# An S4 convolution with a gated GELU block on one core: the y table of a step as one product on VectorE, and a new order of all work

## The chip, the cores and the metric

The kernel runs on one core of a Trainium2 chip. The core has five engines with their own queues: TensorE (PE, matrix products into PSUM), VectorE (DVE), ScalarE (ACT), GpSimd (POOL) and SyncE (SP, which here issues most of the transfers). The metric is the device time of one execution in microseconds (us); lower is better. Three executions of the kernel before took 823.56, 824.63 and 826.21 us, with a median of 824.63 us.

## The reference

An input u of 2048 tokens and 448 channels goes through two blocks, each behind a layer norm that is scaled and shifted by rows computed from a vector c. Cut to what matters:

```python
# S4 block: a convolution kernel per channel, from 256 complex modes
logdA = exp(log_dt)[:, None] * (A_re + 1j * A_im)
P = exp(logdA[:, :, None] * l)                      # l = 0..2047
K = einsum("dn,dnl,dn->dl", Cc, P, dB).real         # 448 x 2048
y = irfft(rfft(u_padded) * rfft(K_padded))[:L] + u * Dskip
x = x + ga * y
# gated block
h = layernorm(x) * (1 + cb) + sb
x = x + gb * ((gelu(h @ w_gate) * (h @ w_up)) @ w_down)
```

The costly part of the first block is K: 448 x 2048 values, each a sum over 256 complex modes of an exponential with a decay and an angle. The costly part of the second is three matrix products of 448 by 1792.

## The kernel before, in words

**The tables of K.** The time l is split as l = 64 l1 + l2. For a mode the power then factors into an x table (over the 32 values of l1) and a y table (over the 64 values of l2); K of a channel is the product of the two, summed over the modes. The work goes in 56 steps of 8 channels. In a step s:

- `exps` (lines 759 to 795) makes the magnitudes: a matrix product and an exponential on ScalarE give `mx` for two steps (line 775) and `my` for one (line 793, 1024 elements: 2 halves of modes, 8 channels, 64 values of l2).
- `angles` (lines 797 to 841) makes sine and cosine. Matrix products of bf16 pieces (line 806) leave the angle in turns, with whole turns taken off by a large constant, in PSUM; ScalarE makes the sine (line 819) and the cosine. In the first 28 steps the cosine comes from a second set of angles with a quarter turn added (`anc`, line 830); in the other 28 it is the sine of the angle's absolute value minus a quarter turn (lines 811 or 814, then 823). Both lie in one tile `fg`, for x and for y. The y angles cover 32 values of l2 only; the other half of the 64 is carried by the two halves of `my` and by signs.
- `mults` (lines 844 to 867) makes the tables on VectorE: `tx` is one product of 1024 elements (line 855). `ty` has three: the cosine part, 1024 elements (line 859), the sine part of the first half with its sign turned, 512 elements (line 862), and the sine part of the second half, 512 elements (line 863).
- `kgen` (lines 871 to 890) has 64 small matrix products, line 886, `tx` as weights and 64 columns of `ty` as the moving operand, into `kg`.
- `ktail` then copies `kg` out into `ke` (`kev`), applies a first stage of the Fourier transform (line 911) and collects the result in `ako` (`kout`). Copies out of PSUM, which may run on ScalarE or VectorE, go through the helper `cp` and show as line 585 (ScalarE) or 587 (VectorE).
- The rows that the products of lines 769, 788 and 806 take as weights come from DRAM for seven steps at a time, by `load_lt` (line 751).

Beside the steps run: the preparation of the modes for four groups of 112 channels (`prep`), the norm and transform of u (`u_norm_a`, `u_stage_b`), and for two of three groups of channels the product of the transforms and its inverse (`k_fft`, lines 1189 to 1213, with constants loaded by line 1181). The third group's transforms (`t_fft`) come after the last step.

**The gated block.** `conv_out` adds the convolution, norms it and transposes it; `gate_up` makes gate and up with fp16 pieces (lines 1588 and 1594), GELU (1601) and the product (1608); `down_first` (line 1663) and `down` (line 1694) make the last product.

**What sets the order.** The program is not written in the order in which it runs. Each piece of work is a `Task` with its engine or engines, a cost in us, the tasks it depends on and the buffers it takes. `Plan.order` is a list planner: it keeps a clock for each engine, finds the engine that can start something first, and gives it, among the tasks that can start by then or shortly after, the one of lowest priority value in `PRIO`. `PRIO` has one number for each of some 2000 tasks. A task with two engines (copies out of PSUM) goes to the one that ends it first. A change of ScalarE's function table costs `TABLE` = 1.3 us in the plan, a hand-over between engines `HOP` = 0.3 us, and all transfers share one pipe of 280 GB/s. The planner runs when the program is built; its result is a fixed order for each engine and each queue, in which each instruction waits for what it needs. So a number in the planner never runs on the chip; it only moves instructions within their queues.

Of the kernel before, what the change touches and what calls it, by code (L numbers as in the profile page):

```python
# [11 lines left out]
FT = mybir.dt.float32  # L12
# [3 lines left out]
AF = mybir.ActivationFunctionType  # L16
OP = mybir.AluOpType
# [20 lines left out]
WS = 256.0  # L38
PRIO = {
    "anc": (-1293.256, -3578.895, -353.961, -872.318, -460.437, -1921.377, -2404.991, -2215.805, 191.288, -32.981, -202.691,  # L40
        -2647.333, -1933.83, -670.792, -192.873, -616.144, -80.921, -1549.964, -2941.687, -671.342, -2001.879, -1132.111,
        -71.643, -27.945, -252.965, -1535.421, -769.379, -1539.333),
    "ang": (-63.859, -7.725, -30.71, 0.169, 7.925, 11.195, 9.268, 21.779, 22.824, 25.594, 26.183, 26.493, 28.144, 28.708,
# [5 lines left out]
    "c.ai": (-2663.528,),  # L49
    "c.ak": (171.218,),  # L50
    "c.au": (-4200.533,),
    "c.c": (-933.544,),
    "c.ea": (5422.27,),
    "c.id": (-147.248,),
    "c.ih": (1109.11,),
    "c.ld": (-3220.083,),
    "c.rd": (2966.135,),
    "co.adde": (-84.218, -1452.145, -2417.83, -1409.323),
    "co.addl": (-57.786, 676.69, 1533.586, 31.466),
    "co.addx": (-1428.076, -8.045, 2531.362, 3088.204, -2578.892, 2089.375, -473.92, 382.232, 1219.977, -537.482, 53.247,  # L60
        1140.208),
    "co.c2": (553.038, 3254.154, 1888.633, -595.169, 1726.527, -906.573, 4858.759, 40.493, -1400.834, 27.831, 1819.503,
        -161.366),
    "co.h": (336.967, 2645.855, 1868.777, -2126.118),
    "co.h2": (-650.973, 75.139, 637.166, -1259.465, -8.18, -1329.599, 13.947, -1333.575, 5413.552, -346.388, 3335.76, 1270.416),
    "co.l": (-2527.984, -675.661, 723.03, 3544.242),
    "co.l2": (1124.467, 1797.664, 1246.234, 626.032, 529.696, 1269.558, 529.646, -451.738, -1181.182, 2221.273, 450.372,
        434.525),
    "co.mme": (4028.037, 3822.614, -709.965, -3597.943),
    "co.mml": (-661.981, 33.929, 1870.772, -68.779),  # L70
    "co.mmx": (348.366, -620.465, 1977.413, 2997.574, -279.998, 3308.134, 630.569, 742.671, -398.692, -288.917, -47.372,
        2601.845),
    "co.n": (-637.705, -78.904, -2172.773, -124.152),
    "co.nx": (-1207.602, 1920.968, -700.888, 0.561, -1307.228, -3639.226, 373.628, -35.065, -24.718, 34.24, 1425.966, -6133.847),
    "co.rc": (1435.224, -2102.468, 1120.167, 435.885),
    "co.rcx": (864.192, -118.249, 3179.105),
    "co.rt": (-668.81, -40.146, 1435.174, -1099.33),
    "co.rtx": (-306.185, -80.314, 5310.55),
    "co.t": (-701.977, -362.858, 11.547, -251.511),
    "co.t2": (-1003.663, 677.507, 490.748, 1973.53, -67.147, -1774.919, -292.344, -677.791, 196.69, -3024.797, -183.214, 15.548),  # L80
    "cos": (47.809, 4338.677, -1916.389, -1985.479, 48.84, 450.345, -228.642, 1373.754, -1635.183, -2125.449, -2951.945,
        139.392, -590.217, -1488.189, -465.57, -115.397, -138.704, 2366.141, 654.971, 78.486, 63.259, -3501.827, 365.129,
        -594.75, 843.446, -2481.552, 3748.658, 338.746),
    "cos2": (-186.283, -458.553, -28.501, -1467.414, -186.383, 305.735, -4173.308, 2676.943, -903.314, -2645.906, -803.054,
        147.233, 61.493, -902.839, -698.019, 3.975, 96.182, 670.288, 4882.18, -890.924, -903.013, 1267.647, -38.519, 1684.391,
        654.047, -1006.703, 490.617, -217.831),
    "d.hi": (-16.935, -885.611, 1072.565, -1866.073, 565.92, -545.207, 277.832),
    "d.ld": (-1036.334, 594.218, -5342.563, -1512.808, 784.13, 1290.275, -992.387),
    "d.lo": (-1950.133, -1401.218, -2174.946, -390.7, -1260.169, -6.416, 1957.309),
    "d0": (-1079.999,),  # L90
    "dn": (-3573.259, -323.838, 1692.909, 1720.273),
    "dn.k0": (1759.554, 521.981, -3993.33),
    "dn.k2": (-1082.302, -1650.584, -6237.94),
    "dn.k3": (-388.073, 2717.888, 2751.692),
    "dn.r": (586.912, 103.145, 2224.364, -500.948),
# [1797 lines left out]
```

## Time and profile before

| | |
|---|---|
| median of three executions | 824.63 us |
| profiled execution | 822.29 us |
| its span, first to last instruction | 820.5 us |
| TensorE busy | 744.8 us, 91% |
| VectorE busy | 609.2 us, 74% |
| ScalarE busy | 464.4 us, 57% |
| mean granted clock of TensorE | 0.972 |
| moved by DMA | 136.78 MB, mean 167 GB/s |

The shares are means over stages with different limits: loads and preparation up to about 40 us, the 56 steps up to about 371 us, the last transforms and the way into the gated block up to about 420 us, and the gated block from there on. A row of the table of stretches gives, for each engine, its busy time in the stretch and the number of instructions; a row of a group gives the line of the program, the engine, what is written and read, the count, the busy time, the mean length of one in ns, and the engine's idle time just ahead with what ended it. The chain that ended last follows the work back from the last instruction, at each step to what released it.

### The profile page before, as it was taken

To read this page: it belongs to the slowest core of one execution; us is meant where nothing else is said; L and a number is where in the kernel's file an instruction comes from. 1 tells how busy PE (TensorE), PEld (TensorE's weight loads), DVE (VectorE), ACT (ScalarE), POOL (GpSimd) and SP (SyncE) were. 2 spreads that over 40 slices of the span, in tenths; PEclk is the share of its full clock that TensorE was granted. 3 is DMA by queue.
4 is the path that set the end of the run, shared out by engine and by line. 5 is a ranking of instruction groups with operands and counts; after the bars stand their busy time and mean duration, and the time that the engine had idled before them with its cause. 6 is when DMAs were issued, how large, how long until landed. Compare 5 with 4: busy or idle time off the path is not lost.

```text
span 820.5 us, 19136 instructions
## 1 busy us (share of the span) xinstructions
PE 744.8 (91%) x8172; PEld 455.8 (56%) x8172; DVE 609.2 (74%) x1034; ACT 464.4 (57%) x610; POOL 11.1 (1%) x28
## 2 busy tenths in 40 slices
PE   0787788989899999988689999999999999999997
PEld 0333344443577766678566445444496445954477
DVE  5799999898989999996875783178884655744552
ACT  4598998999899999880245551034332233223320
POOL 1000000000000000001200000000000000000000
PEclk9879999999999999999879999999999999999999
DMA  9644459997967755989769641644416232012101
GB/s 266 161 147 138 116 145 246 282 261 234 221 198 223 224 160 165 295 276 279 242 224 310 234 158 63 162 150 139 135 53 185 77 127 96 24 68 90 45 13 35
DMA packets 92839, 136.78 MB, mean 167 GB/s; under 512 B 22672, under 2 KB 75184, under 8 KB 92754
## 3 DMA queue, kind: packets, MB, share of 16 engines
q1 hardware_dynamic: 86480, 131.02, 52.6%
q10 hardware_dynamic: 5458, 3.12, 1.3%
q8 instruction: 64, 1.05, 0.5%
q0 software_dynamic: 816, 1.42, 0.5%
q14 instruction: 21, 0.17, 0.1%
HBM read 100.42 MB, written 36.01 MB: 166 GB/s over the span
## 4 chain that ended last, share of the span: by engine, by line
PE 62%; ACT 14%; DVE 9%; DMA 8%; issue 5%; SPq 2%; ACTq 0%; DVEq 0%
PE pq L1594 30%; PE pq L1694 8%; PE pd L1663 4%; ACT fg L819 3%; PE kg L886 3%; DMA u_d<-so 2%; PE pg L806 2%; ACT my L793 2%; PE pq L1588 2%; PE pf L1205 2%; PE pf L1103 2%; PE pd L1694 1%; DMA fg<-in_w_mod 1%; DVE ty L859 1%; ACT fg L811 1%
## 5 line engine op out<-in xcount | busy, mean ns | idle before, releaser
L1594 PE MATMUL pq<-ht,wr 128*128 128x512 f16 (+1 forms) x1200 | 248.7, 365 | 0.0
L1594 PEld LDWEIGHTS <-wr 128*128 128x128 f16 x1200 | 114.4, 98 | 128.9 <-issue 12.3
L1608 DVE TENSOR_TENSOR fq<-ge,pq 128x512 f32<-128x512 f32 (+1 forms) x60 | 39.0, 651 | 83.4 <-PE pq L1594 58.5
L1601 ACT ACTIVATE ge<-pq 128x512 f32<-128x512 f32 (+1 forms) x60 | 34.0, 567 | 113.8 <-PE pq L1588 69.4
L1620 ACT ACTIVATE hh<-fq 128x1024 f16<-128x1024 f32 (+1 forms) x49 | 47.2, 964 | 59.9 <-DVE fq L1608 44.5
L886 PE MATMUL kg<-ty,tx 128*32 128x64 f32 x3584 | 63.6, 224 | 13.4 <-DVE ty L863 9.0
L886 PEld LDWEIGHTS kg<-ty,tx 128*32 128x32 f32 x3584 | 54.4, 112 | 32.7 <-DVE ty L863 14.0
L855 DVE TENSOR_TENSOR tx<-mx,fg 128x1024 f32<-128x1024 f32 x56 | 67.3, 1215 | 2.8 <-ACT fg L830 2.8
L1694 PE MATMUL pq<-d,hh 128*128 128x224 f16 x476 | 69.3, 259 | 0.0
L859 DVE TENSOR_TENSOR ty<-my,fg 128x1024 f32<-128x1024 f32 x56 | 67.9, 1216 | 1.7 <-ACT fg L823 1.7
L1694 PE MATMUL pq<-d,hlo 128*128 128x224 f16 x238 | 61.6, 259 | 0.0
L819 ACT ACTIVATE fg<-pg 128x1024 f32<-128x1024 f32 x56 | 57.7, 1032 | 3.5 <-issue 1.5
L793 ACT ACTIVATE my<-pg 128x1024 f32<-128x1024 f32 x56 | 55.9, 1037 | 5.6 <-PE pg L788 5.1
L1623 DVE TENSOR_TENSOR hlo<-fq,hh 128x1024 f16<-128x1024 f32 (+1 forms) x49 | 53.6, 1103 | 3.1 <-ACT hh L1620 3.1
L1694 PEld LDWEIGHTS <-hh 128*128 128x128 f16 x560 | 53.9, 98 | 0.8 <-issue 0.3
L1205 PE MATMUL pf<-q,fc 128*128 128x160 f32 x264 | 41.8, 307 | 0.2
L806 PEld LDWEIGHTS <-lt 64*128 64x128 bf16 x336 | 19.3, 94 | 40.0 <-issue 26.0
L1205 PEld LDWEIGHTS pf<-q,fc 128*128 128x128 f32 x264 | 36.6, 190 | 6.2 <-issue 3.4
L806 PE MATMUL pg<-ea,lt 64*128 64x512 bf16 x168 | 33.1, 387 | 6.7 <-ACT fg L819 5.2
L863 DVE TENSOR_TENSOR ty<-my,fg 128x512 f32<-128x512 f32 x56 | 38.2, 682 | 0.0
L862 DVE SCALAR_TENSOR_TENSOR ty<-my,fg 128x512 f32<-128x512 f32 x56 | 38.1, 681 | 0.0
L911 PE MATMUL kg<-ak,ke 128*64 128x128 f32 x448 | 30.6, 279 | 3.7 <-issue 2.0
(198 smaller groups left out, 1207.2 us busy)
## 6 DMA issues: line engine op xcount, KB each, us to landing
wr<-w_d SPq DMA_DIRECT2D x21, 896.0 KB, 4.6
fc<-in_k_fc SPq DMA_DIRECT2D x20, 576.0 KB, 5.2
u_d<-so SPq DMA_DIRECT2D x32, 224.0 KB, 4.5
w<-in_wgu SPq DMA_DIRECT2D x14, 512.0 KB, 4.1
ui<-u_d SPq DMA_DIRECT2D x10, 672.0 KB, 6.2
w_d<-wr SPq DMA_DIRECT2D x7, 896.0 KB, 7.1
fq<-in_wd SPq DMA_DIRECT2D x14, 448.0 KB, 3.8
us<-uo SPq DMA_DIRECT2D x22, 240.0 KB, 6.5
```

The source lines that it names most:

```text
L793: A.activation(yb.tile.rearrange("p a b c -> p (a b c)"), pb.tile, AF.Exp)
L806: T.matmul(pa[:, nh * 512:nh * 512 + 512], w, x, start=(k == 0), stop=(k == 2))
L819: A.activation(fb.tile[:, 0].rearrange("p x (n k) -> p n x k", n=2), pb.tile.rearrange("p (n x k) -> p n x k", n=2, x=2), AF.Sin, scale=TW ...
L855: V.tensor_mul(tx.tile, xb.tile[:, xm, None, :].to_broadcast([128, 2, 512]), fb.tile[:, :, 0])
L859: V.tensor_mul(ty.tile[:, 1], yb.tile, fy()[:, 1, :, None, :].to_broadcast([128, 16, 2, 32]))
L886: T.matmul(kg[32 * g:32 * g + 32, 2 * (s % 2) + q, :64], tx[:, r, nh, 4 * q + g], ty[:, r, nh, 4 * q + g], start=(r == 0 and nh == 0), sto ...
L1205: T.matmul(pz.tile[:, e % 32 - sl0], fc.tile[:, i, 1 + t], pp.tile[:, t, i], start=(t == 0 and e != 32), stop=(t == 1 and e != 0))
L1594: T.matmul(pb.tile[k][:, ts], wr.tile[:, 4 * lo + t, k, c0:c0 + 128], ht[:, m, ts], start=f % 2 == 0 and i == 0, stop=f % 2 == 1 and i == 9)
L1608: V.tensor_mul(to if half is None else to[:, half:half + 1], *src)
L1620: A.activation(hg.tile[0][:, cb, c], fq.tile[:, c], AF.Copy)
L1623: V.tensor_sub(hg.tile[1][:, cb, c], fq.tile[:, c], hg.tile[0][:, cb, c])
L1694: T.matmul(bank(k)[:, m], x[:, p, q[0], ts], w[:, p, q[1]], start=new and m == 0 and p == 0 and z == 0, skip_group_check=True, stop=i in ( ...
```

## The change

**The y table.** All angles, those of x and those of y, are turned by an eighth of a turn: row 6 of each channel's rows in the constant `ea` holds -0.125 for the sine's angles and -0.375 for the second set, and the row of ones that they multiply (`k_one`) is zero in the copy that the exponentials read. With the turn the two parts of the y table need no sign of their own, so `ty` becomes one product of 2048 elements: each half of `my` times both sine and cosine. `kgen` picks the pairs that it needs with a slice (1 and 2, or 0 and 3) for the moving operand. `my` is laid out by halves of l2, so the exponential of line 793 writes in runs of 256 elements. The absolute-value cosine changes the sign of its scale and bias.

**The order.** The planner's costs are scaled, for each kind of work and engine, by a new table `PACE`; the hand-over cost depends on the two engines (`HOPS`, 0.04 to 0.2 us), on buffers 0.15 us and behind a transfer 0.25 us; 21 kinds of work (`INTURN`) are kept in the order of their steps by a dependency on the one before of the same kind; the three queues of transfers have a clock each and share the rate while two are busy. Every number in `PRIO` is new.

```diff
+PACE = {
+    ("anc", "PE"): 0.97, ("ang", "PE"): 0.87, ("bn", "DVE"): 1.12, ("co.adde", "DVE"): 1.06, ("co.addx", "DVE"): 1.04,
...
+    ("gu.s", "DVE"): 1.05, ("gu2", "PE"): 0.96, ("ka", "PE"): 0.98, ("kev", "ACT"): 0.82, ("kev", "DVE"): 0.82,
...
 PRIO = {
...
     TABLE, HOP, STICK, BIAS, RATE = 1.3, 0.3, 103.13, -0.27, 280.0
+    HOPD, HOPB = 0.25, 0.15
+    HOPS = {("PE", "ACT"): 0.2, ("PE", "DVE"): 0.2, ("ACT", "DVE"): 0.04, ("DVE", "ACT"): 0.1, ("DVE", "PE"): 0.13, ("ACT", "PE"): 0.15}
+    INTURN = ("ang", "tx", "tyc", "x.mm", "y.mm", "x.exp", "y.exp", "f.ut", "f.fc", "f.fwd", "f.inv", "lt0", "lt1", "ub.u", "ub.fc", "ub", "kev", "ka",
+              "t.fwd", "t.inv", "wr.ld")
...
+        eng = {e: c * PACE.get((n, e), 1.0) for e, c in eng.items()}
+        if n in self.INTURN:
+            deps = list(deps) + [self.last.get(n)]
...
-                    s = max(sl + self.HOP if sl else 0.0, free.get(e, 0.0))
+                    s = max(sl + self.HOPB if sl else 0.0, free.get(e, 0.0))
                     for d in t.deps:
-                        x = d.end if d.on == e and not d.kb else d.end + self.HOP
+                        x = d.end + (self.HOPD if d.kb else 0.0 if d.on == e else self.HOPS.get((d.on, e), self.HOP))
...
             if t.kb:
-                dma = max(dma, t.end) + t.kb / self.RATE
-                t.end = max(t.end + 2.0, dma + 1.5)
+                s0, w = max(dq[e], t.end), t.kb / self.RATE
+                x = min(w, max(0.0, max(y for q, y in dq.items() if q != e) - s0))
+                for q in dq:
+                    if q != e and dq[q] > s0:
+                        dq[q] += x
+                dq[e] = s0 + w + x
+                t.end = max(t.end + 2.0, dq[e] + 1.5)
...
-        ea[:, 8 * c + 6, 1024 + c * 32:1024 + (c + 1) * 32] = 0.25
-        ea[:, 8 * c + 6, 1280 + c * 32:1280 + (c + 1) * 32] = 0.25
-    ea[:, :, 1024:] += ea[:, :, :512]
+    ea[:, :, 1024:] = ea[:, :, :512]
+    for c in range(8):
+        for z in (0, 256):
+            ea[:, 8 * c + 6, z + c * 32:z + (c + 1) * 32] = -0.125
+            ea[:, 8 * c + 6, 1024 + z + c * 32:1024 + z + (c + 1) * 32] = -0.375
...
-        "k_one": np.ones((4, 2, DT, 2, N), ml_dtypes.bfloat16),
+        "k_one": one,
...
-    V.memset(halfpi, -0.5 * math.pi)
+    V.memset(halfpi, 0.5 * math.pi)
...
-                    yb.tile = tabl.tile([128, 16, 2, 32], FT, name="my", bufs=NMY)
-                    A.activation(yb.tile.rearrange("p a b c -> p (a b c)"), pb.tile, AF.Exp)
+                    yb.tile = tabl.tile([128, 2, 512], FT, name="my", bufs=NMY)
+                    A.activation(yb.tile.rearrange("p h (n k) -> p n h k", n=2), pb.tile.rearrange("p (n h k) -> p n h k", n=2, h=2), AF.Exp)
...
-            A.activation(fb.tile[:, 1], fb.tile[:, 1], AF.Sin, scale=TWO_PI, bias=halfpi)
+            A.activation(fb.tile[:, 1], fb.tile[:, 1], AF.Sin, scale=-TWO_PI, bias=halfpi)
...
-        def fc_():
-            ty.tile = tab.tile([128, 2, 16, 2, 32], FT, name="ty")
-            V.tensor_mul(ty.tile[:, 1], yb.tile, fy()[:, 1, :, None, :].to_broadcast([128, 16, 2, 32]))
-
-        def fs():
-            V.scalar_tensor_tensor(ty.tile[:, 0, :, 0], yb.tile[:, :, 0], -1.0, fy()[:, 0], op0=OP.mult, op1=OP.mult)
-            V.tensor_mul(ty.tile[:, 0, :, 1], yb.tile[:, :, 1], fy()[:, 0])
+        def fy():
+            ty.tile = tab.tile([128, 2, 2, 512], FT, name="ty")
+            V.tensor_mul(ty.tile, yb.tile[:, :, None, :].to_broadcast([128, 2, 2, 512]),
+                         fb.tile[:, None, :, 1].to_broadcast([128, 2, 2, 512]))
         x = add("tx", {"DVE": 1.13}, s - 0.4, fx, [si, co, xt_], [tx], [fb, xb])
-        y = add("tyc", {"DVE": 1.13}, s - 0.4, fc_, [co, yt_], [ty], [fb, yb])
-        z = add("tys", {"DVE": 1.2}, s - 0.4, fs, [si, y], (), [fb, yb, ty])
-        return x, y, z
+        y = add("tyc", {"DVE": 2.21}, s - 0.4, fy, [si, co, yt_], [ty], [fb, yb])
+        return x, y
...
-            ty = TY[s].tile.rearrange("p r (n c) h k -> p r n c h k", n=2)
+            ty = TY[s].tile.rearrange("p h t (n c k) -> p (h t) n c k", n=2, k=32)
...
-                                     ty[:, r, nh, 4 * q + g], start=(r == 0 and nh == 0), stop=(r == 1 and nh == 1),
+                                     ty[:, 0:4:3, nh, 4 * q + g] if r else ty[:, 1:3, nh, 4 * q + g], start=(r == 0 and nh == 0), stop=(r == 1 and nh == 1),
```

More of the change, by code (lines that the diff above doesn't have):

```diff
@@ L344, in __init__ @@
         self.slots, self.given = slots, {t: [] for t in slots}
-        self.tasks, self.seen = [], {}
+        self.tasks, self.seen, self.last = [], {}, {}
     def add(self, n, eng, v, fn, deps=(), alloc=(), use=(), table=None, kb=0.0):
         i = self.seen[n] = self.seen.get(n, -1) + 1
-        t = Task(n, eng, PRIO[n][i] if i < len(PRIO.get(n, ())) else v, fn, [d for d in deps if d is not None], alloc, table, kb)
+        eng = {e: c * PACE.get((n, e), 1.0) for e, c in eng.items()}
+        if n in self.INTURN:
+            deps = list(deps) + [self.last.get(n)]
+        t = self.last[n] = Task(n, eng, PRIO[n][i] if i < len(PRIO.get(n, ())) else v, fn, [d for d in deps if d is not None], alloc, table, kb)
         for d in t.deps:
@@ L371, in order @@
     def order(self):
-        free, table, dma, out = {}, None, 0.0, []
+        free, table, out = {}, None, []
+        dq = dict.fromkeys(("SP", "ACT", "POOL"), 0.0)
         lane = {"SP": [-1e9] * 8, "POOL": [-1e9] * 8}
```

419 lines of the change are left out of this document (218 added, 201 removed), and 152 rows, old and new, of tables (PACE, PRIO).

## The prediction

> **What bounds the kernel now.** I read the table of stretches first, then the groups of instructions, then the chain that ended last, and last the order of time on VectorE. The profiled execution took 822.3 us, 1.8 us more than its span of 820.5 us; the median of the three runs, 824.6 us, is 2.3 us above it. Sums below are made against 822.3 us, and 2.3 us are added at the end.
>
> The stretches, with the busy time of each engine and its count of instructions:
> ```profile
> core 0: us, PE busy (x) PEld busy (x) DVE busy (x) ACT busy (x) POOL busy (x), PEclk, DMA share, GB/s
> ...
> 40.00:120.00 80.00, 63.95 (x952) 33.03 (x956) 77.81 (x136) 72.09 (x97) 0.00 (x0) 0.89 0.46 133
> 120.00:200.00 80.00, 71.28 (x1091) 34.28 (x1079) 71.81 (x131) 74.08 (x108) 0.00 (x0) 0.98 0.92 263
> 200.00:280.00 80.00, 77.44 (x1514) 53.94 (x1514) 75.78 (x108) 75.79 (x89) 0.00 (x0) 1.00 0.76 215
> 280.00:371.00 91.00, 83.32 (x1742) 63.43 (x1738) 85.93 (x121) 82.13 (x97) 0.00 (x0) 1.00 0.72 222
> 371.00:420.00 49.00, 37.04 (x279) 32.67 (x280) 37.09 (x71) 8.97 (x14) 7.94 (x14) 0.83 0.77 236
> 420.00:820.00 400.00, 395.09 (x2571) 230.83 (x2569) 234.77 (x410) 130.23 (x176) 0.00 (x0) 1.00 0.37 119
> ```
> From 420 us on TensorE is busy 395 of 400 us at a granted clock of 1.00: the gated stage is TensorE's work, the change takes none of it away, and a new order can win there at most the 5 us of idleness. The 56 steps of the tables lie between 40 and 371 us. There VectorE is busy 311.3 of 331 us (77.81 + 71.81 + 75.78 + 85.93), ScalarE 304.1 and TensorE 296.0. So no engine alone sets that stage: VectorE has 19.7 us of slack, ScalarE 26.9 us, TensorE 35.0 us. Work taken from VectorE shortens it only so far as ScalarE gives work over in turn.
>
> The chain that ended last says the same; two pieces of it inside the stage, and the pieces between the stages:
> ```profile
> 208.51 6.89 DMA fc<-in_k_fc
> ...
> 217.15 1.21 DVE ty L859
> ...
> 369.61 12.81 issue
> ...
> 386.93 5.47 DMA my<-in_k_fc
> ...
> 404.92 3.90 DMA w<-in_wgu
> ```
> The chain passes from engine to engine and through loads; after 371 us it is a tail of hand-overs and transfers in which the y tables have no part any more.
>
> **The change part by part.** First the y table. The four products of a step, by lines, all 56 steps:
> ```profile
> L859 DVE TENSOR_TENSOR ty<-my,fg 128x1024 f32<-128x1024 f32 x56 | 67.9, 1216 | 1.7 <-ACT fg L823 1.7
> L855 DVE TENSOR_TENSOR tx<-mx,fg 128x1024 f32<-128x1024 f32 x56 | 67.3, 1215 | 2.8 <-ACT fg L830 2.8
> L863 DVE TENSOR_TENSOR ty<-my,fg 128x512 f32<-128x512 f32 x56 | 38.2, 682 | 0.0
> L862 DVE SCALAR_TENSOR_TENSOR ty<-my,fg 128x512 f32<-128x512 f32 x56 | 38.1, 681 | 0.0
> ```
> Lines 859, 862 and 863 go (144.2 us of durations), and one product of 2048 elements comes. Durations overstate what an instruction costs, since the next one starts before the record ends. VectorE in order of time, where nothing waits:
> ```profile
> 343.79 1.22 DVE L859 TENSOR_TENSOR ty<-my,fg 128x1024 f32<-128x1024 f32 x1
> 344.92 0.68 DVE L862 SCALAR_TENSOR_TENSOR ty<-my,fg 128x512 f32<-128x512 f32 x1
> 345.52 0.68 DVE L863 TENSOR_TENSOR ty<-my,fg 128x512 f32<-128x512 f32 x1
> 346.13 2.35 DVE L855 TENSOR_TENSOR tx<-mx,fg 128x1024 f32<-128x1024 f32 x2
> ```
> From start to start the 1024 elements take 1.13 us and each half of 512 takes 0.60 to 0.61: the three cost 2.34 us. 512 elements more cost 0.525 us, so the part that does not grow is 0.08 us, and 2048 elements cost 0.08 + 4 x 0.525 = 2.18 us from start to start. The saving is 0.16 us a step at the middle; with starts rounded to 0.01 us it lies between 0.12 and 0.18. I take 0.15: 56 x 0.15 = 8.4 us of VectorE (6.7 to 10.1). The new record itself should last 1.216 + 2 x (1.216 - 0.682) = 2.28 us.
>
> [...]
>
> How much of the 8.4 us is on the path? If VectorE alone set the stage, all of it; if it were hidden, nothing. VectorE and ScalarE are within 7 us of each other, and the planner may put copies on either of them (13 copies of line 587 into uo take 8.1 us on VectorE, 20 of line 585 take 10.7 us on ScalarE):
> ```profile
> L587 DVE COPY uo<-pf 128x448 f32<-128x448 f32 x13 | 8.1, 619 | 1.6 <-PE pf L1103 1.2
> L585 ACT ACTIVATE uo<-pf 128x448 f32<-128x448 f32 x20 | 10.7, 564 | 0.4 <-PE pf L1103 0.4
> ```
> So a saving on one becomes half a saving on both: I take 4.2 us on the path, ends 0 and 10.1.
>
> The other edits of the arithmetic. The exponential of y writes in runs of 256 elements; line 775 already does:
> ```profile
> L775 ACT ACTIVATE mx<-pg x32: 580/1024/1092, 37.5 to 335.5; 128x1024 f32<-128x1024 f32 x24, 128x512 f32<-128x512 f32 x8
> L793 ACT ACTIVATE my<-pg 128x1024 f32<-128x1024 f32 x56 | 55.9, 1037 | 5.6 <-PE pg L788 5.1
> ```
> A median of 1024 ns against a mean of 1037: nothing, 0 to -0.7 us. The matrix products of line 886 read the y table as two runs, 1 or 3 halves apart, instead of one run of 64. The nearest row is line 1663, whose moving operand is picked by the same two slices:
> ```profile
> 493.40 15.89 PE pd L1663 x84
> ...
> 530.49 8.74 PE pq L1594 x40
> ```
> 84 products of 448 columns in 15.89 us are 0.422 ns a column; 40 of 512 in 8.74 us with one run are 0.427. So nothing; with another type and shorter runs I leave 0 to +10% on 63.6 us of TensorE's line 886, 6.4 us, of which the stage's 35 us of slack on TensorE hides most. The eighth of a turn sits in a row of the constants that the angle products read anyway: same matmuls, no instruction more. The cosine's scale and bias only change sign. The loads of constants keep their size.
>
> One product waits for both the sine and the cosine and holds VectorE 2.18 us at a stretch. The matrix product of a step waits for it at the head of TensorE's order:
> ```profile
> PEld kg L886 <- DVE ty L863: 14.0, 13, 2.6
> PE kg L886 <- DVE ty L863: 9.0, 10, 2.4
> ```
> It waited for the last half of the table in 13 of 56 steps already, and behind it stand the angle products that feed ScalarE. In the three pieces other copies can be slipped in between, now not; a copy that comes up at the wrong moment waits up to 1.05 us longer (2.18 - 1.13). One in ten of 56 would be 6 us of one engine's waits, 0 on the path while the other two have work ready. I take 0, ends 0 and +3.
>
> Second, the order. All instructions of all engines and queues are placed anew by the list planner, with costs scaled to measured spacing, shorter hand-overs, a rule that keeps 21 kinds of work in turn, and DMA queues that share the rate. Where old and new prices can be compared, the new ones are nearer to this trace. The copy into ke was priced at 0.32 us on ScalarE and is now at 0.26:
> ```profile
> 358.61 0.39 ACT L585 ACTIVATE ke<-kg 128x252 f32<-128x252 f32 x1
> 358.87 1.16 ACT L823 ACTIVATE fg<-fg,small 128x1024 f32<-128x1024 f32 x1
> ```
> 0.26 us from start to start. A hand-over from VectorE to TensorE was 0.30 us and is 0.13:
> ```profile
> 212.47 0.68 DVE L863 TENSOR_TENSOR ty<-my,fg 128x512 f32<-128x512 f32 x1
> 213.21 0.94 PEld L886 LDWEIGHTS kg<-ty,tx 128*32 128x32 f32 x64 [0.62 <-DVE ty L863]
> ```
> The half-table's 0.60 us end at 213.07, the weights start at 213.21: 0.14 us. A plan made with prices that hold leaves fewer holes. There are 19.7 us of them on VectorE and 26.9 on ScalarE, 23 in the mean. I let the new order close a quarter, 6 us. That is a choice: below it nothing, above it half of them (12 us) and 5 us of the waits between 371 and 420 us.
>
> The new order may also change the number of table loads on ScalarE:
> ```profile
> L819 ACT ACT_TABLE_LOAD x9 | 11.5, 1283 | 0.2
> L793 ACT ACT_TABLE_LOAD x6 | 7.7, 1283 | 0.2
> L775 ACT ACT_TABLE_LOAD x6 | 7.7, 1283 | 0.1
> ...
> 213.16 1.28 ACT L793 ACT_TABLE_LOAD   x1
> ...
> 214.45 1.94 ACT L793 ACTIVATE my<-pg 128x1024 f32<-128x1024 f32 x2
> ```
> 21 of them belong to the switches between exponentials and sines; five more or fewer are 6.4 us of ScalarE, half of it on the path. I take no change.
>
> The sum: 822.3 - 4.2 - 6.0 = 812.1 us profiled, 814.4 us as a median.
>
> **The rivals.** A change under 0.3% of 824.6 us (2.5 us) is about what a measurement of this kernel cannot tell from none.
>
> The order gains nothing, and only the product does: -4.2 us, 820 us. For it: the order before was searched as well, and its engines are 92 to 94% busy. Against it: 23 us of holes.
>
> The saving is hidden altogether: ScalarE, busy 304.1 of 331 us, sets the stage and gives nothing over, and the order is as good as the old one. 824 us. For it: the sines and exponentials can run nowhere else. Against it: the copies of line 585 can.
>
> [...]
>
> Slower: the load queue. SP issues its loads in the planned order, and one that waits for its buffer holds all behind it:
> ```profile
> SPq L1181 <- PE pf L1205: 43.0, 14, 8.9
> SPq L751 <- DMA lh_d<-lh: 21.1, 3, 17.3
> ```
> Line 1181 (the constants of the transforms) waits 43 us in 14 issues, up to 8.9, mostly with nothing urgent behind it; once, at 208.5 us, it cost 6.89 us on the chain. The new planner models a load of the same kind as waiting for the one before to land, a wait that the program itself does not contain, so its idea of when buffers come free and what stands behind a waiting load can be off. If such a load stands ahead of the table rows of the next seven steps (line 751), sines, products and matrix products all run dry. Two more such waits are 13.8 us; against them stand 4.2 us, the order wins nothing: 824.6 + 13.8 - 4.2 = 834 us. It decides from 10.2 us on, one and a half such waits. For it: DMA is already 0.92 busy from 120 to 200 us. Against it: the buffers and the sizes stay.
>
> **How the numbers follow.** Forecast (product and order) 0.48, 814.4 us; product alone 0.16, 820 us; durations as the price 0.03, 810 us; hidden 0.10, 824 us; load queue 0.23, 834 us. Faster by over 0.3% is 0.48 + 0.16 + 0.03 = 0.67, within 0.3% 0.10, slower 0.23. The forecast's own range is 803 to 820 us: below, half of the holes (12 us) with the 4.2 us and 5 us of the waits after 371 us give 803; above, it meets the product alone. The whole range is 802 to 831: a tenth is left below for the full 10.1 us with a tighter order, a tenth above for the longer cases of the load queue.
>
> **What would show it.** Right: one product of 2048 elements on VectorE, 56 times, at 2.28 us, its successor 2.18 us after its start; VectorE's sum 15 to 17 us of durations lower, the last matrix product of line 886's kind about 10 us earlier than 371 us, the gated stage still some 395 us of TensorE. Wrong: VectorE's hole grows by the 8 us that it saved; matrix products waiting on the y table for more than the 23 us above; more than 26 table loads on exponentials and sines; a load wait over 7 us on the chain in the stage; or a stretch after the last table of more than 49 us.

## The result and the profile after

The changed kernel takes 830.68 us, median of eight runs (827.88 to 832.94), beside 825.12 us for the kernel before on the same chip: ratio 1.0063, 95% interval 1.0042 to 1.0084. It is slower by 0.6%, twice the 0.3% that the prediction took as the least difference to be told from none. The forecast was 814.4 us and faster; the time lies at the upper edge of the range.

The profiled execution has a span of 828.7 us (820.5 before), mean granted clock 0.965 (0.972 before). First the groups of the two table products after, and VectorE in order of time:

```profile
L897 DVE TENSOR_TENSOR ty<-my,fg 128x2048 f32<-128x2048 f32 x56 | 126.9, 2285 | 1.8 <-PE kg L920 1.3 <-ACT fg L864 0.4
L893 DVE TENSOR_TENSOR tx<-mx,fg 128x1024 f32<-128x1024 f32 x56 | 67.3, 1218 | 5.9 <-PE kg L920 2.5 <-ACT fg L871 2.3 <-issue 0.7
```
```profile
301.74 2.28 DVE L897 TENSOR_TENSOR ty<-my,fg 128x2048 f32<-128x2048 f32 x1
303.94 1.22 DVE L855 TENSOR_SCALAR fg<-pg 128x1024 int32<-128x1024 int32 x1
```

The product is what the prediction made of it: 2.28 us long, the next instruction 2.20 us behind its start (2.18 was worked out), and 126.9 us in all where the three took 144.2.

The table of stretches after, with the stage of the tables in one row:

```profile
core 0: us, PE busy (x) PEld busy (x) DVE busy (x) ACT busy (x) POOL busy (x), PEclk, DMA share, GB/s
0.00:40.00 40.00, 16.02 (x42) 7.46 (x44) 27.05 (x67) 17.68 (x29) 3.14 (x14) 0.92 0.81 219
40.00:371.00 331.00, 291.42 (x5100) 179.91 (x5096) 302.55 (x369) 303.60 (x386) 0.00 (x0) 0.95 0.70 202
371.00:430.00 59.00, 44.62 (x473) 39.22 (x466) 42.81 (x77) 15.64 (x26) 8.58 (x15) 0.85 0.74 225
430.00:828.00 398.00, 395.23 (x2572) 231.17 (x2572) 239.05 (x421) 121.83 (x162) 0.00 (x0) 1.00 0.38 120
```

VectorE is busy 302.6 us there, 8.8 us less than before (311.3), and nothing came of it. But this row ends at 371 us, and the tables end later than that, so it leaves out their last steps. TensorE's gated stage is 395 us as before. The loss is made before 380 us. The last products of the kernel generator, in order of time, before and after:

```profile
368.79 2.14 PE L886 MATMUL kg<-ty,tx 128*32 128x64 f32 x128 [1.34 <-DVE tx L855]
```
```profile
377.33 2.12 PE L920 MATMUL kg<-ty,tx 128*32 128x64 f32 x128
```

They end at 370.9 us before and at 379.4 us after; what follows takes 449.6 us before and 449.3 after. So the whole 8.2 us by which the spans differ lie in the tables, and the study is about the 380 us ahead of that row. Below, "the tables end at" means the end of that row, each time in one profile. Counted from 40 us to there, VectorE is busy 311.3 us before and 309.4 after, and idle 19.6 and 30.0. Over the whole execution the changed kernel has even more for VectorE to do: 611.4 us, 609.2 before, and less for ScalarE (458.8, 464.4 before), since the new order gives some copies and magnitudes to another engine.

What TensorE waits for in the stage changed. The longest rows of the view of its waits between 40 and 371 us (total in us, times, longest), after:

```profile
PE pg L829 <- ACT my L834: 5.9, 8, 1.6
PE pg L847 <- ACT fg L860: 3.6, 5, 1.3
PE pg L829 <- ACT mx L816: 3.0, 5, 1.4
PE pg L847 <- ACT fg L871: 3.0, 1, 3.0
PE kg L920 <- issue: 2.7, 2, 1.8
PE pg L829 <- ACT fg L871: 2.6, 2, 1.9
PE kg L920 <- DVE ty L897: 2.5, 3, 1.1
```

and before:

```profile
PE kg L886 <- DVE ty L863: 9.0, 10, 2.4
PE pg L806 <- ACT fg L819: 5.2, 8, 1.5
PE pf L1040 <- DVE xt L1031: 3.9, 2, 2.9
PE kg L886 <- DVE tx L855: 2.9, 2, 1.5
...
PE pg L788 <- ACT my L793: 1.4, 3, 0.7
```

The wait of the kernel generator for the y table fell from 9.0 to 2.5 us: there the relief arrived. In its place TensorE stands at the products of the angles and magnitudes (lines 829 and 847) until ScalarE has read the PSUM pair that they write. Summed over all rows of that view, TensorE waits 7.2 us for VectorE (19.6 before) and 25.3 us for ScalarE (12.5 before).

### The profile page after: what moved, and what is told of

It reads as the page before. It is cut to its first block, busy times and chain, and to the rows that moved or that the text cites. A ratio compares the mean times of both kernels' runs of the same rounds, so it can differ in the third digit from the quotient of the medians.

```text
span 828.7 us, 19024 instructions
## 1 busy us (share of the span) xinstructions
PE 747.3 (90%) x8172; PEld 457.8 (55%) x8172; DVE 611.4 (74%) x931; ACT 458.8 (55%) x602; POOL 11.7 (1%) x29
## 3 DMA queue, kind: packets, MB, share of 16 engines
q8 instruction: 64, 1.05, 0.5%
## 4 chain that ended last, share of the span: by engine, by line
PE 64%; ACT 16%; DVE 8%; DMA 7%; issue 4%; SPq 1%; ACTq 0%; DVEq 0%; POOLq 0%
PE pq L1628 30%; PE pq L1728 8%; PE pd L1697 4%; PE kg L920 3%; DVE ty L897 2%; ACT fg L860 2%; ACT my L834 2%; DMA fg<-in_w_mod 2%; PE pg L847 2%; PE pq L1622 2%; PE pf L1326 2%; PE pf L1239 2%; ACT mx L816 2%; PE pd L1728 1%; PE pf L1137 1%
## 5 line engine op out<-in xcount | busy, mean ns | idle before, releaser
L897 DVE TENSOR_TENSOR ty<-my,fg 128x2048 f32<-128x2048 f32 x56 | 126.9, 2285 | 1.8 <-PE kg L920 1.3
L920 PEld LDWEIGHTS kg<-ty,tx 128*32 128x32 f32 x3584 | 55.7, 114 | 22.9 <-issue 10.5
L834 ACT ACTIVATE my<-pg 128x1024 f32<-128x1024 f32 x56 | 55.3, 1041 | 2.8 <-PE pg L829 2.5
L847 PE MATMUL pg<-ea,rd 64*128 64x512 bf16 x168 | 34.3, 391 | 1.2 <-issue 1.2
L847 PE MATMUL pg<-rd,lt 64*128 64x512 bf16 x168 | 34.1, 391 | 0.0
```

The source lines that it names most:

```text
L834: A.activation(yb.tile.rearrange("p h (n k) -> p n h k", n=2), pb.tile.rearrange("p (n h k) -> p n h k", n=2, h=2), AF.Exp)
L847: T.matmul(pa[:, nh * 512:nh * 512 + 512], w, x, start=(k == 0), stop=(k == 2))
L897: V.tensor_mul(ty.tile, yb.tile[:, :, None, :].to_broadcast([128, 2, 2, 512]), fb.tile[:, None, :, 1].to_broadcast([128, 2, 2, 512]))
L920: T.matmul(kg[32 * g:32 * g + 32, 2 * (s % 2) + q, :64], tx[:, r, nh, 4 * q + g], ty[:, 0:4:3, nh, 4 * q + g] if r else ty[:, 1:3, nh, 4 * ...
```

## The experiments

The change has two halves, the arithmetic and the order. A kernel can be given any order of tasks, with the engine of each task, as a list in place of the planner. Call the orders "old" (of the kernel before) and "new" (of the changed kernel). Theory A: the product gains some us and the new order loses more than that. Theory B, the prediction's rival: the saving is hidden, and the order is what decides. All ratios are to the kernel before, run beside it on the same chip.

**Order and arithmetic apart (e1, e2).** In e1 the changed arithmetic runs in the old order; in e2 the three products run in the new order.

```diff
     def order(self):
-        ... (list planner)
+        out = sorted(self.tasks, key=lambda t: RANK[t.n][t.i])
+        for t in out:
+            t.on = ON[t.n].split()[t.i]
+        return out
```

> One product of 2048 elements per step, as changed, but every task in the order of the kernel before and on the engine that it had there; the product stands where the last half of the table stood. Theory A (the new order is what costs): VectorE has 56 x 0.13 to 0.16 = 7 to 9 us less to do and nothing else moves, so the time falls by 1 to 5 us below the kernel before, ratio 0.994 to 0.999. Theory B (the long product or the strided read of the table costs, the order is neutral): the time is that of the changed kernel or near it, ratio 1.004 to 1.008.

> The arithmetic of the kernel before (three products per step), in the order of the changed kernel, the two halves of 512 directly behind the product of 1024. Theory A: slower than the changed kernel, by up to the 7 to 9 us that VectorE has more to do, ratio to the kernel before 1.007 to 1.017. Theory B: back to the kernel before or better, ratio 0.995 to 1.002.

e1: 827.06 us, ratio 1.0034 (1.0006 to 1.0061), tables end at 374.6 us. e2: 830.94 us, ratio 1.0093 (1.0061 to 1.0125), tables end at 381.3 us. The row of the stage for e1:

```profile
40.00:371.00 331.00, 298.49 (x5160) 184.98 (x5157) 304.31 (x380) 304.61 (x388) 0.00 (x0) 0.95 0.71 206
```

VectorE is busy 7.0 us less than before (311.3) in that stretch and 6.4 us less over the whole execution (602.8 and 609.2), and the kernel isn't faster. Between e2 and the changed kernel, where both have the new order, the product takes 6.2 us from VectorE (617.6 and 611.4). So the saving exists, and nothing of it reaches the end in e1. The new order costs 0.9% with the old arithmetic, as theory A has it. With the new arithmetic it costs less, 0.3% (1.0034 to 1.0063), and there the two intervals overlap. And e1 fits neither theory: A asked for 0.994 to 0.999, B for 1.004 to 1.008. Why e1 is even 0.3% slower than the kernel before isn't shown. In its profile 2 us of the 3.7 by which its tables end later come from its first load of `w_mod`, which lasted 13.94 us in the chain and 11.97 us in the profile of the kernel before. That load varies among profiles that begin with the old order (12.01 us in e3, 13.77 in e5), so these 2 us may be chance.

**Is it the block of 2.2 us? (e3)** The old order with two products of 1024 elements at the two old places.

```diff
-            V.tensor_mul(ty.tile, yb.tile[:, :, None, :]..., fb.tile[:, None, :, 1]...)
+            V.tensor_mul(ty.tile[:, 0], yb.tile[:, 0, None, :]..., fb.tile[:, :, 1])
+        def fz():
+            V.tensor_mul(ty.tile[:, 1], yb.tile[:, 1, None, :]..., fb.tile[:, :, 1])
```

> The order of the kernel before, task by task and engine by engine, with the angles of the changed kernel, but the y table as two products of 1024 elements at the two places where the kernel before had its one and its pair (one pair of places, of step 49, moved behind a sine). VectorE's work on it is about as long as with one product, in two pieces. Theory 'block': the piece of 2.2 us on VectorE, in a queue whose other work TensorE and ScalarE wait for, ate the 7 us that VectorE was relieved of with one product in the old order; in two pieces they come back, 818 to 823 us where the kernel before has 824. Rival 'hidden': VectorE's relief lies beside ScalarE and TensorE in any form: 824 to 828, like the one product in the old order (827).

826.13 us, ratio 1.0013 (0.9995 to 1.0031), tables end at 372.8 us. The intervals of e1 and e3 overlap. The block isn't what ate the saving: two short pieces do no better than the kernel before either. That the block costs up to 0.2%, the distance of e1 from e3, isn't excluded.

**Where in the order? (e4, e5, e6)** Two hybrids, cut behind the kernel generator of step 26, and the new order with the old choice of engine for 75 copies and magnitudes.

```diff
+    pre = P[:P.index(("kgen", 26)) + 1]          # e4: P new, S old; e5: P old, S new
+    order = pre + [t for t in S if t not in pre]
-    ON = {...}                                   # e6: engines of the new order
+    ON = {...}                                   # e6: engines of the old order for 75 tasks
```

> The changed kernel's arithmetic, in its new order up to the kernel generator's matmuls of step 26 (about 227 us), then the rest in the old order with the old choice of engines. Theory 'second half': the new order loses its time behind step 26, where it gives VectorE more of the magnitudes and copies; then this kernel stays within 3 us of the old order with one product, 824 to 828. Theory 'no slack': the new order loses everywhere by small slips that it can't give back, 827 to 830, half way.

> The mirror image: the old order up to the matmuls of step 26 (about 232 us), then the new order with its choice of engines. Theory 'second half': the whole loss is here, 829 to 833. Theory 'no slack': half of it, 827 to 830.

> The changed kernel in its new order, but the 75 copies and magnitudes of the tables and the prologue that the new order gave to another engine back on the one that the kernel before used. Theory 'engines': the loss comes from the magnitudes and copies that VectorE was given; 824 to 827. Theory 'no slack': the sequence is what costs, 829 to 833.

e4: 838.38 us, 1.0167 (1.0139 to 1.0195). e5: 831.53 us, 1.0058 (1.0032 to 1.0085). e6: 848.33 us, 1.0258 (1.0210 to 1.0306). e5 alone fits the second half as the culprit; e4 contradicts it, since with the old second half it is slower than either parent. Its generator takes 21.1 us from step 26 to step 28, where the new order takes 15.6 and the kernel before 7.3: the hybrid loses at its own seam. Of the engines e6 says that they belong to the sequence: put back, they make the new order 1.9% worse. These three don't place the loss; they say that a piece of one plan isn't worth what it was worth in the whole.

**How much does a slip of TensorE cost? (e7, e8)** The generator's 64 products are issued twice in nine steps, in both orders; the second pass overwrites the first with the same values.

```diff
-            for q in range(2):
+            for q in (0, 1, 0, 1) if s in (6, 10, 14, 18, 22, 26, 30, 34, 38) else (0, 1):
```

> The changed kernel in its new order, with the 64 matmuls of the kernel generator issued twice in nine steps (6, 10, 14 and so on to 38): nine pieces of 1.03 us at full clock, 9.3 us in all, are added on TensorE, which has some 35 us of idle time in this stage. Theory 'no slack': nearly every slip of TensorE in the new order reaches the end, 5 to 9 us on the changed kernel's 830.7, 836 to 840. Rival 'a few bad places': the new order is as elastic as the old one and loses at a few places only; then the piece costs as much here as in the old order.

> The old order with one product (827.1), with the same nine matmul groups doubled, 9.3 us of TensorE at full clock. Theory 'no slack': the old order gives such slips back, 0 to 4 us more, 827 to 831. Rival 'a few bad places': the same addition as in the new order. If both gain little or get faster, TensorE's added work was paid back by a higher granted clock: in the new order more of it, since there the granted clock is lower (0.87 between 80 and 120 us against 0.96).

e7: 852.16 us, 1.0334 (1.0271 to 1.0397), 21.5 us above the changed kernel. e8: 836.97 us, 1.0141 (1.0089 to 1.0193), 9.9 us above e1. Both are more than expected, and the new order pays over twice as much. But part of it is a wait that neither theory had counted; TensorE in e7, in order of time:

```profile
184.34 2.37 PE L940 MATMUL kg<-ty,tx 128*32 128x64 f32 x153
191.73 1.29 PE L940 MATMUL kg<-ty,tx 128*32 128x64 f32 x39 [5.03 <-issue]
```

In the middle of 192 products in a row TensorE stands for 5.03 us and waits for nothing that the view of waits names. Such waits at the generator come to 12.7 us in e7 and 4.7 us in e8. The changed kernel has 2.7 us of them and e1 0.3. With the difference taken off, e7 costs about 11 us for the 9.3 added and e8 about 5: the new order has less room for TensorE's slips than the old one. That this wait adds up so simply is assumed, not shown. What the traces show at such stops is in the last section: in the changed kernel each ends 1.4 to 1.5 us after a packet of q8, the DMA queue of the kind "instruction", has landed.

**Is it TensorE's clock? (e9 to e13)** In the trace TensorE's granted clock falls to 0.50 at some of the holes in its work (in the kernel before from 126 to 129 us, where a hole of 2.37 us ends at 126.57 us), and the changed kernel is longer at half clock (mean 0.965 against 0.972 of the span). Dummy products were put into the holes.

```diff
         for t in self.order():
+            if (t.n, t.i) in FILL:
+                filler(FILL[t.n, t.i])   # n products ak x ak into columns 64 to 127 of a kg tile
```

> The kernel before, unchanged but for dummy matmuls (256 columns into the unused half of a kernel-generator tile, 128 columns into outputs that are overwritten next) in front of nine places of its TensorE queue between 30 and 130 us and of two in the transition (402 to 413 us), where its trace shows TensorE idle for 0.8 to 6.6 us and the granted clock at a half just after. Theory 'clock': each hole costs twice, since TensorE runs the 3 to 16 us behind it at half clock; filled, the half-clock time falls, and the kernel gets 2 to 7 us faster: 817 to 822. Rival 'the clock is beside the point': ScalarE and VectorE set the pace in 40 to 371 us, and dummies that overrun their hole only delay: 823 to 828.

> The changed kernel with dummy matmuls in the same manner at its own holes (thirteen places between 30 and 126 us, two in the transition). Theory 'clock': its loss against the old order is the 12 us more that TensorE spent at half clock (mean 0.965 against 0.972); filled, the gap to the kernel before with its holes filled closes to under 2 us: 818 to 823. Theory 'no slack': the order stays slower by 4 us or more than the filled kernel before, 825 to 831.

e9: 856.05 us, 1.0371 (1.0322 to 1.0419). e10: 860.95 us, 1.0431 (1.0374 to 1.0488). The clock rose to 0.996 and 0.992, and the dummies overran their holes: one took 0.45 us (in e9 the 101 dummies of 256 columns are 202 records, 45.9 us busy), four times what I had reckoned. So the same with a fourth of them, and in the transition alone:

> As e9, with the dummies at a fourth of their number, since the 128x256 dummy took 0.45 us in e9 where 0.11 had been reckoned: 21 of them in front of nine places (9.5 us), and 22 and 8 of 0.23 us in the two holes of the transition. Theory 'clock': half-clock time falls with little delay, 817 to 823. Rival: 823 to 829.

> The kernel before with dummies in the transition alone (22 in the hole of 6.6 us at 402 us, 8 in that of 2.5 us at 411 us). Theory 'clock': the transposes and the first gated products behind the hole, which ran at 0.50 up to 419 us in the kernel before, run at full clock, and the first full-width gated product starts 2 to 4 us earlier: 820 to 823. Rival: the dummies hold up what waits behind them: 824 to 827.

> As e10 with the short dummies: 26 of 0.45 us at fourteen places between 30 and 126 us, 17 and 8 of 0.23 us in the transition. Theory 'clock' (the order's loss is TensorE's half-clock time): 819 to 825, level with the short-filled kernel before. Theory 'no slack': work added on TensorE costs more here than in the old order, 828 to 840, 5 us or more above the short-filled kernel before.

e11: 824.97 us, 0.9978 (0.9953 to 1.0003). e12: 822.80 us, 0.9960 (0.9935 to 0.9985). e13: 826.96 us, 1.0018 (0.9986 to 1.0050). The stretch from 80 to 120 us in e13:

```profile
80.00:120.00 40.00, 36.00 (x586) 20.28 (x582) 39.14 (x50) 37.94 (x49) 0.00 (x0) 1.00 0.38 107
```

The granted clock is 1.00 there (0.87 in the changed kernel) and its mean 0.990; still the tables end at 378.6 us, 0.8 us earlier than without dummies, and in e11 at 374.4 us, 3.5 us later than before. So the higher clock didn't bring the new order's tables back, with the dummies' own 12 us of TensorE in the price; what the clock alone is worth these runs can't say, since it comes only with that work. With both orders filled the distance is smaller: 0.4% between e11 and e13, whose intervals overlap, where it was 0.6%, and 4.2 us between the ends of their tables, where it was 8.5. So a part of the loss may be the clock; the ends of the tables, in one profile each, speak against its being all. e13's own gain lies behind the tables (444.6 us in place of 449.3). e12 fills the hole in the transition only; before, and in e12:

```profile
402.00:414.00 12.00, 2.95 (x23) 2.30 (x20) 9.37 (x26) 3.21 (x6) 1.70 (x3) 0.66 0.77 255
414.00:420.00 6.00, 6.00 (x32) 4.47 (x32) 4.72 (x9) 1.20 (x2) 0.00 (x0) 0.55 0.15 36
```
```profile
402.00:414.00 12.00, 10.29 (x91) 8.53 (x91) 8.93 (x23) 3.19 (x5) 2.30 (x4) 1.00 0.79 255
414.00:420.00 6.00, 4.16 (x34) 3.06 (x33) 5.89 (x14) 2.44 (x4) 0.00 (x0) 1.00 0.24 98
```

The clock stays at 1.00 through the transposes. In the medians that is 0.4%; in its one profile the part behind the tables takes 449.7 us, no less than before, so the gain isn't seen there. In the kernel before the clock falls to 0.50 at about 406 us, inside the hole of 6.6 us that begins at 402 us, and stays there for 13.6 us.

**Is it the head of TensorE's queue? (e14, e15)** Twelve tasks whose inputs were ready are issued ahead of the neighbour at which TensorE stood; in e15 five swaps of that kind in the old order, with e12's dummies.

```diff
-    ..., y.mm 7, ua 11, ..., ang 46, f.fwd 13, ...
+    ..., ua 11, y.mm 7, ..., f.fwd 13, ang 46, ...
```

> The changed kernel in its new order, with twelve tasks of TensorE's queue (two groups of the blocked transforms at about 55 and 92 us and one at 94, kernel-generator tails at 140 and 325, transforms at 148, 180, 226, 231, 266, 294 and 314 us) issued ahead of a neighbour that TensorE stood at for 0.5 to 3.0 us in the changed kernel's trace while those twelve had all their inputs. Nothing else moves, and no work is added or left out. Theory 'head of the queue': the new order loses because TensorE, which takes its queue in order, stands at tables' products whose PSUM pair ScalarE still reads (its waits for ScalarE in 40 to 371 us are 25.3 us against 12.5 before) with ready work behind them; the twelve give 3 to 7 us back: 824 to 828. Rival 'engines': the waits only move to the next place, 829 to 832.

> The kernel before with the dummies of e12 in the transition and five tasks of TensorE's queue swapped with a blocked neighbour in the same way (transforms at about 104, 195, 217, 310 and 345 us). If the head of the queue is what the old order loses by as well, 1 to 3 us below e12 (822.8, 0.996 of the kernel before): 0.993 to 0.996. If not, 0.996 to 0.998.

e14: 834.27 us, 1.0117 (1.0083 to 1.0152), tables end at 384.4 us: slower than the changed kernel (1.0063) by half a per cent. e15: 824.83 us, 0.9989 (0.9962 to 1.0016). So these twelve stops weren't free time. TensorE's waits for ScalarE between 40 and 371 us fell from 25.3 to 23.8 us, ScalarE's for TensorE rose from 17.9 to 21.8. I read it so: a transform of 1 us put into a stop of 0.5 us makes the product behind it later, and ScalarE waits for that product. e15 also doesn't repeat e12's 0.4%, so I don't call e12 a proven gain.

**What paces a step? (e16, e17, e18)** The y product on half of its elements, in the new and in the old order, and ScalarE's exponential of y on half of its elements in the new order. Each leaves out half of the y table, or of its magnitudes, and reads the other half twice.

```diff
-            V.tensor_mul(ty.tile, yb.tile[:, :, None, :]..., fb.tile[:, None, :, 1]...)
+            V.tensor_mul(ty.tile[:, 0], yb.tile[:, 0, None, :]..., fb.tile[:, :, 1])   # e16, e18
-            A.activation(yb.tile..., pb.tile..., AF.Exp)
+            A.activation(yb.tile[:, 0]..., pb.tile...[:, :, 0], AF.Exp)                # e17
```

> The changed kernel in its new order, with the y product on half of its elements (1024 in place of 2048; the kernel generator reads that half twice, so half of the y table is left out). VectorE is relieved of some 1.07 us (2.29 less the 1.22 of the x product) in each of 56 steps, 60 us, seven times what the change itself saved. Theory 'ScalarE and TensorE pace': VectorE isn't what the steps wait for, 0 to 8 us faster than the changed kernel (830.7): 823 to 831. Rival, the prediction's joint bound: half of it reaches the end, 30 us, about 801.

> The changed kernel in its new order, with ScalarE's exponential of the y table on half of its elements (512 in place of 1024; the product reads that half twice, so the other half of the factor is left out). ScalarE is relieved of some 0.4 us in each of 56 steps, 23 us. Theory 'ScalarE and TensorE pace': half or more reaches the end, 12 to 23 us, 808 to 819. Rival joint bound: the same half of a saving as for VectorE, 12 us. If neither this nor the half product moves the time, TensorE alone paces.

> The half product of e16 in the old order with one product (827.1). Theory 'ScalarE and TensorE pace' here too: 0 to 8 us faster, 819 to 827. Rival: VectorE paces the old order (TensorE's waits for VectorE are 18.5 us in its tables against 7.2 in the new order), 15 to 30 us faster: 797 to 812; then the product's saving was too small or came at the wrong place to be seen, and not hidden.

e16: 829.18 us, 1.0038 (1.0014 to 1.0063). e17: 827.92 us, 1.0036 (1.0005 to 1.0067). e18: 818.50 us, 0.9911 (0.9882 to 0.9941). The rows of the stage, one each for e16, e17 and e18:

```profile
40.00:371.00 331.00, 290.76 (x5098) 179.03 (x5095) 248.63 (x369) 303.22 (x386) 0.00 (x0) 0.95 0.69 203
```
```profile
40.00:371.00 331.00, 293.22 (x5098) 180.48 (x5095) 302.10 (x369) 281.77 (x386) 0.00 (x0) 0.94 0.69 202
```
```profile
40.00:371.00 331.00, 301.21 (x5309) 189.94 (x5310) 250.96 (x383) 302.94 (x388) 0.00 (x0) 0.96 0.72 214
```

In the new order 53.9 us less on VectorE (302.55 to 248.63; 56.8 over the whole execution) are worth 2 us (0.25% of 825), 4 in a hundred; 21.8 us less on ScalarE (303.60 to 281.77; 21.2 over the whole) are worth about as much, 10 in a hundred. The intervals of both overlap with that of the changed kernel. In the old order 53.4 us less on VectorE (304.31 to 250.96; 55.7 over the whole) are worth 10.1 us (1.0034 to 0.9911), 18 in a hundred of the whole. So VectorE hardly paces the new order, and the old one by a fifth. e17 is a miss: half or more of ScalarE's 23 us was expected at the end. By its expectation TensorE alone would then pace; e7 fits that, but no run takes work from TensorE. Where ScalarE is relieved, it waits for TensorE in turn; the longest rows of ScalarE's waits in e17:

```profile
ACT my L854 <- PE pg L849: 6.8, 9, 1.7
ACT ke L646 <- PE kg L940: 6.6, 7, 3.6
ACT mx L836 <- PE pg L830: 6.2, 7, 1.6
ACT ako L646 <- PE kg L965: 5.5, 6, 1.5
```

Over all rows that is 41.4 us against 17.9 in the changed kernel, while TensorE still waits 20.9 us for ScalarE. With the sequence fixed, the hand-overs between TensorE and ScalarE go on in their turn, and what an engine saves it stands idle.

## Why the prediction was wrong

**Right.** The size of the product (2.28 us, successor 2.20 us later, sum 17.3 us of durations lower) and about that of VectorE's saving: 8.4 us were worked out, 6.7 at the least, and e1 shows 6.4 over the whole execution. The rows came nearer than the durations, as the successor at 2.20 us under a record of 2.28 shows again. That durations are the price, to which the prediction's chances give 0.03, no run shows. The other edits cost nothing that shows: the exponential of y takes 1041 ns (1037 before), line 920 is 65.0 us of TensorE (63.6 before), and the table loads on exponentials and sines are 24 (23 before, by the same lines; the prediction counted 21 and left out the 2 of line 823). The block costs at most little (e1 and e3). The gated stage is the same.

**Wrong: "a saving on one becomes half a saving on both", 4.2 us on the path.** The step reasoned from busy shares: VectorE 311 and ScalarE 304 of 331 us, so joint bounds between which the planner evens out. In these fixed orders nothing evened out. By e18 a fifth of a large saving on VectorE reaches the end in the old order; if a small one went the same way, that would be 1.2 us of the 6.4, which no measurement here can show. By e16 next to nothing does in the new one. Between e2 and the changed kernel, the same order with three products and with one, lie 0.3%, within the width of the intervals. The rival that the saving is hidden, to which I gave 0.10, is nearest to what the arithmetic did. The sign that I named, VectorE's hole growing by what it saved, is clear in e1, where it grew from 19.6 to 27.9 us up to the end of the tables; in the changed kernel it grew to 30.0, mostly because the tables end later.

**Wrong: "I let the new order close a quarter" of the holes, 6 us.** The new order loses about 7.7 us with the old arithmetic (e2, 0.9%); together with the new arithmetic the loss is 5.2 us, of which 2.4 are left against the old order with that arithmetic (e1). I took two prices that were nearer to the trace as a sign that the plan would hold. But holes on the engines aren't a reserve that a nearer price list can fetch: in e16 and e17 the holes on VectorE and ScalarE were made far larger, and the tables ended at 377.9 and 379.0 us all the same. Why the plan with the closer prices lost is open. That it kept less room is the best reading: work added on TensorE costs it twice what it costs the old order (e7, e8).

**The rival on the load queue** gave the right sign and nearly the time (834 us), by a mechanism that isn't seen. The chain after passes through loads longer than 7 us:

```profile
133.24 8.17 DMA fg<-in_w_mod
...
157.94 7.65 DMA fu<-in_k_fc
...
221.38 9.77 DMA fg<-in_w_mod
```

That was the sign I named. Yet TensorE waited 1.6 us in all for `w_mod` in the stage, in two waits, and SP stood before the constants (line 1215) for TensorE 29.0 us in 7 issues, where it was 43.0 in 14. e3, in the old order and level with the kernel before, has a load of `w_mod` of 9.73 us on its chain too. A long load on the chain says which event came last, not that it held up work.

**What stays open.** That the order costs the time is shown for the old arithmetic (e2). That it isn't the product is shown by e2 as well, and that it isn't the load on VectorE or ScalarE by e16 and e17. The block (e3, in the old order alone), the clock (e11 and e13) and the stops at the head of TensorE's queue (e14, twelve of them) each had a run that speaks against them, but a part may be theirs. Which hand-overs make the 8.5 us isn't shown. Between 40 and 371 us the view of waits has 62 of ScalarE and TensorE for each other, 0.7 us long in the mean and 3.0 at most; they sum to 43.2 us, 29.1 before. That these are the loss is likely, and the hybrids couldn't cut them apart.

## What to carry to other kernels

Before pricing a saving on an engine, ask what share of a saving reaches the end in the given order; one run that halves the work there gives an idea of it (here 4 to 18%), and busy shares don't. A new order and a new arithmetic are two changes: replay each with the other's half before believing either. A plan that is tighter by its own prices may have less slack for what the prices don't know, so test it with a small delay.

## What was unexpected of the hardware

TensorE stopped in the middle of rows of short products. In e7 it stood for 5.03 us after 153 products of 64 columns in a row, and the changed kernel has a smaller case; in order of time:

```profile
364.64 1.09 PE L920 MATMUL kg<-ty,tx 128*32 128x64 f32 x63 [0.44 <-DVE ty L897]
367.54 0.22 PE L920 MATMUL kg<-ty,tx 128*32 128x64 f32 x1 [1.81 <-issue]
```

One product of 64 is left over, 1.81 us late. All such waits of TensorE in the stage are 3.9 us after, 1.3 before, 0.3 in e1 and 14.9 in e7. The page of each profile has a DMA queue of the kind "instruction"; in the changed kernel and in e7:

```profile
q8 instruction: 64, 1.05, 0.5%
```
```profile
q8 instruction: 68, 1.11, 0.5%
```

Each of its packets has 16384 bytes in the changed kernel (64 packets, 1.05 MB). TensorE's products and weight loads are 16344 there and 17496 in e7, about 256 to a packet; by this estimate the queue brings TensorE's instructions. The trace has the time of each packet. Between 40 and 371 us the three stops of the changed kernel and the two of the kernel before all end 1.3 to 1.5 us after such a packet has landed. At the longest, the one above, TensorE stopped at 365.73 us, the packet that had started at 364.99 landed at 366.18, and TensorE went on at 367.54. That TensorE had run out of instructions is how I read these times; no run shows it alone, and that the longer stops of e7 are of the same kind is assumed. Why a packet comes late isn't shown. These stops alone are not the new order's loss: e2 has 1.9 us of them and ends its tables at 381.3 us, e13 shows none in the stage and ends them at 378.6.

The second surprise is the clock: raised from 0.87 to 1.00 over 40 us of the tables, with dummies of 12 us put in, it left their end where it was to 0.8 us.
